# Output projection in 256-wide operands, partial sums added off TensorE, and one unit for the value products

## The chip, the cores and the metric

The kernel runs on one core of a Trainium2 chip. The metric is the device time of one execution in microseconds: the median of three runs, with the lowest and the highest beside it. TensorE (PE) does the matmuls, VectorE (DVE), ScalarE (ACT) and GpSimd (POOL) the elementwise work, and SyncE (SP) issues nearly all DMAs.

## The reference

Two attention layers over the same 2048 x 512 input `x` (bf16), mixed row by row by a gate. Layer A is a recurrence over 64 segments of 32 tokens; layer B is causal attention inside four blocks of 512 tokens, with a running memory.

```python
g = sigmoid((x * gate_w).sum(-1, keepdims=True))

# A: 32 heads of 128, M = 8 memory rows, seg_len = 32
mem = mem0
for s in range(64):
    h = concat([mem, x[:, 32*s : 32*s + 32]], axis=1)     # 40 rows of 512
    q, k, v = h @ Wq, h @ Wk, h @ Wv                      # 32 heads x 128
    p = softmax(where(mask, q @ k.T * 128**-0.5, -1e9))   # 40 x 40 a head
    o = einsum('bhte,hed->btd', p @ v, Wo)                # 40 rows of 512
    mem = o[:, :8]
    outs.append(o[:, 8:])
a = concat(outs)

# B: 32 heads of 16, blocks of 512 tokens, softmax attention plus a linear memory
b = (...) @ wo
out = g * a + (1 - g) * b
```

The 40 rows of a segment are the eight memory rows and its 32 tokens; the first eight rows of the segment's output are the memory of the next one. So the segments of A can only run one after the other.

## The kernel before

`build` (L258) records operations for each engine in the order in which Python emits them, and `Prog.emit` (L211) turns the recorded reads and writes into semaphore waits. Each engine runs its own list in order. For layer A the order is written out by hand: sixteen lists `A_LIST0` to `A_LIST15`, one for each group of four segments, in which a word such as `2.K0x` is one unit of work of segment 2 of the group. `plan_a` (L1275) makes the units and runs the lists.

A segment's TensorE work has 32 columns: its eight memory rows and its first 24 tokens, held in `hT` (two buffers, one a segment; GpSimd copies the tokens in, `x_copy`, L1554). The last eight tokens of four segments are 32 more columns, done once a group from `xL` (`left_units`, L1327; `ol_units`, L1422); no later segment needs them early. With 32 columns a matmul uses a quarter of the array's columns, so four matmuls run side by side, on row quarters `SEG * j` of one PSUM bank.

Units of one segment, in the order in which they depend on each other (`b` is 0 or 1, one half of the 32 heads):

- `K`, `Q`, `V` + `b` + `x` or `y` (`nat_pass`, L1566, matmuls at L1305): the projections, 512 columns a matmul, eight matmuls a unit; `x` needs the first half of the memory rows in `hT`, `y` the second. `k`, `q`, `v` copy them out of PSUM, `TK`, `TQ` transpose them on VectorE (L1317).
- `S` (L1592): the scores, `X` exp on ACT, `Y` the mask on VectorE, `M` the sums of each row by a matmul with ones (L1633), `L` logarithm and exp on ACT for the reciprocal (L1640, L1643), `N` and `n` the normalising on VectorE and GpSimd (L1647, L1653).
- `PV`, `PL` (L1656, L1669): the value products of one half, into two pairs of banks, for the segment's own tokens and for the left ones. `E` + `b` + `a` or `b` copies two banks at a time to `OT_sb` (L1681).
- `W` + `b` + `a` or `b` (`wo`, L1690): Wo, eight matmuls of 512 columns a unit (`out_part`, L1386, matmuls at L1392). Each of the four row quarters of the bank sums other heads, so four partial sums of 32 rows x 512 stand in one bank.
- `H0`, `H1` copy the halves of the bank to `WF` in float32; `F0`, `F1` (`fold`, L1403, matmuls at L1410) add the four partial sums and transpose them by a float32 matmul with a stacked identity; `hm0`, `hm1` (L1705) copy the memory columns to the other `hT`, `ax0`, `ax1` (L1711) the other columns to `aT_st`. At the end of a group VectorE transposes `aT_st` into rows, and four DMAs store them in DRAM (L1463).

Layer B (`BAttn`, L869) and the last quarter of its projections (`LateB`, L789) are cut into small units too (`bS` scores, `bE` exp and mask, `bP` values, `bT` the end of a job, `pj` and `pp` late projections), and these and the units of the left tokens stand between the units of A. The tail units `tb`, `tf` (L1482) load A's rows back, make B's rows (L1505) and store `g * a + (1 - g) * b`. SP issues the loads for B (`load`, L889), the stores and the tail's loads from one queue in order.

PSUM has eight banks. `Banks` (L43) hands them out while the list is run; `pair` gives two neighbours, and where no bank is free, `relief` runs a pending unit first.

Of the kernel before, what the change touches and what calls it, by code (L numbers as in the profile page):

```python
# [42 lines left out]
class Banks:  # L43
# [3 lines left out]
    def __init__(self, res):  # L47
        self.free = list(range(len(res)))
        self.res = res
        self.oldest = True  # L50
        self.relief = lambda: False

    def take(self, long=False):
        while not self.free and self.relief():
            pass
        assert self.free, "out of banks"
        f = self.free
        if long:
            c = [b for b in f if b < 2] or f
        elif self.oldest:  # L60
            c = [b for b in f if b > 1] or f
        else:
            whole = [b for b in f if b > 1 and b ^ 1 in f]
            c = [b for b in f if b not in whole and b > 1] if len(whole) <= 4 else [b for b in f if b > 1]
            c = c or [b for b in f if b > 1] or f
        b = c[0]
        f.remove(b)
        return b

    def pair(self):  # L70

        found = lambda: [(max(self.free.index(b), self.free.index(b + 1)), b) for b in self.free if b % 2 == 0 and b + 1 in self.free]
        while not found() and self.relief():
            pass
        c = found()
        c = [x for x in c if x[1] > 1] or c
        assert c, "no two neighbouring banks"
        b = min(c)[1]
        self.free = [k for k in self.free if k not in (b, b + 1)]
        return [b, b + 1]  # L80
# [177 lines left out]
def build(nc, es, A_x, A_mem0, A_Wq, A_Wk, A_Wv, A_Wo, B_wq, B_wk, B_wv, B_wo, B_beta, gate_w, out, dbg=None):  # L258
# [31 lines left out]
    def alloc(stack, *specs):  # L290
        at, spans = 0, {}
        for name, shape, dt, n in specs:
# [10 lines left out]
    alloc(es, ("ident", [128, 128], BF16, 0), ("xT", [128, C, S], BF16, 0), ("hT", [128, C, SEG], BF16, 2),  # L303
          ("Wk_sb", [128, C, HE], BF16, 0), ("Wq_sb", [128, C, HE], BF16, 0), ("Wv_sb", [128, C, HE], BF16, 0),
          ("Wo_sb", [128, H, DM], BF16, 0), ("woB_sb", [128, C, DM], BF16, 0),
          ("gw_sb", [128, C], BF16, 0), ("g_sb", [128, NTT], F32, 0), ("omg_sb", [128, NTT], F32, 0),
# [6 lines left out]
          ("aTg", [128, C, 128], BF16, 0), ("fold", [128, SEG], F32, 0), ("VNL", [128, 2, 512], BF16, 0),  # L313
          ("WF", [128, DM], F32, 0))
    esP = ExitStack()
    in_p = alloc(esP, ("wkB", [128, C, DM], BF16, 0), ("wqB", [128, C, DM], BF16, 0), ("phK", [128, 4, DM], BF16, 0), ("etmp", [128, 512], BF16, 5),
# [4 lines left out]
    v.x_sb = v.Wo_sb[:, 0:NTT, :]  # L321
    v.wvB = v.woB_sb
# [7 lines left out]
          ("oTt", [128, 16, 32], F32, 0), ("t1_sb", [128, DM], F32, 0), ("aT_st", [128, C, 128], BF16, 2))  # L330
# [11 lines left out]
    dram("aTd", [NG, 128, DM])  # L342
# [4 lines left out]
    def Rs(name):  # L347
        if name not in R:
            R[name] = Res(name)
            home = v.home(name)  # L350
            if home:
# [5 lines left out]
             ("QT", "QT_sb"), ("VN", "V_sb"), ("Pn", "P_sb"), ("P0", "P_sb"), ("P1", "P_sb"), ("R0", "R_sb"), ("R1", "R_sb"), ("OTL", "OTL"),  # L357
             ("OT", "OT_sb"), ("oTt", "oTt"), ("t1", "t1_sb"), ("aT", "aT_st"))

    def late_home(name):  # L360
        if name.startswith(("aTd", "aTg", "PT")):
# [4 lines left out]
        return h + name[3] if h == "aT_st" else h  # L366
# [27 lines left out]
    v.g_out = [P.group("out%d" % i, "out") for i in range(NG)]  # L394

# [32 lines left out]
    v.BK.oldest = False  # L428
    v.BK.free = sorted(v.BK.free)
    plan_a(v, NSEG_RUN)  # L430
    for go in v.g_out:
# [9 lines left out]
def plan_const(v):  # L441
# [29 lines left out]
    def late():  # L471
# [7 lines left out]
        rf = Rs("fold")  # L479
        gp(lambda g: g.memset(v.fold[:], 0.0), rf, "fold0", True)  # L480
        for j in range(4):
            sel(v.fold[:], [[-1, SEG]], ALU.not_equal, 1.0, -SEG * j, 1, rf, "fold1_%d" % j)
# [17 lines left out]
def plan_warm(v):  # L500
    P, Rs, BK = v.P, v.Rs, v.BK
    v.warm = v.WF[:, :].bitcast(BF16)[:, 0:512]
# [12 lines left out]
def plan_loads(v, A_x, A_mem0, A_Wq, A_Wk, A_Wv, B_wq, B_wk, B_wv, B_wo, B_beta, gate_w):  # L515
# [35 lines left out]
    def wo(q):  # L551
        P.dma(v.grp("Wo%d" % (q // 2)), lambda s: s.dma_start(v.Wo_sb[:, 4 * q:4 * q + 4, :], wosrc[:, 4 * q:4 * q + 4, :]),
              writes=[Rs("Wo%d" % (q // 2))] + ([Rs("x_sb%d%d" % (q, h)) for h in range(2)] if q < 4 else []), name="dma_Wo%d" % q)
# [70 lines left out]
def gate_parts(v):  # L624
# [4 lines left out]
    def dots(k):  # L629
# [4 lines left out]
        def f_gate(pe):  # L634
            ins = None
            for i in range(4 * k, 4 * k + 4):
                for c in range(C):
                    ins = pe.matmul(v.pb[bk][:, i:i + 1], v.xT[:, c, i * 128:(i + 1) * 128], v.gw_sb[:, c:c + 1],
                                    start=(c == 0), stop=(c == C - 1), skip_group_check=True)
            return ins  # L640
        P.op("pe", f_gate, reads=x_res(v, k) + [Rs("gw")], writes=[v.rbank[bk]], name="gate_mm%d" % k)
        if k == NTT // 4 - 1:
            sigmoid(v, v.pb[bk][:, 0:NTT], v.g_sb, v.omg_sb, "g", [v.rbank[bk]])
            BK.give(bk)

    def memory():
# [8 lines left out]
        v.evac("dve", v.hT[0][:, :, 0:v.M], v.pb16[bk][:, 0:C * v.M].rearrange("p (c t) -> p c t", t=v.M), [bk], [Rs("hTm0_0"), Rs("hTm0_1")], "memT0")  # L655
# [133 lines left out]
class LateB:  # L789
# [25 lines left out]
    def project(self):  # L815
# [23 lines left out]
        P.op("pe", f, reads=x_res(v, v.NB - 1) + [Rs("wvB" if m == "V" else "woc%d" % (k % 4))], writes=[v.rbank[bk]], name="lp%d_%d" % (k, half))  # L839
# [4 lines left out]
    def finish(self):  # L844
# [9 lines left out]
        if k == 0:  # L854
            P.op("gp", lambda g: g.memset(self.vst[:, :, 16:17], 1.0), writes=[Rs("t1")], name="v17l")
# [3 lines left out]
                  self.vst[:, :, 0:16].rearrange("p (e m) d -> p m e d", e=2), "t1", "vd%d_%d" % (sb, i)),  # L859
# [9 lines left out]
class BAttn:  # L869
# [45 lines left out]
    def scores(self):  # L915
# [8 lines left out]
        bks = v.BK.pair() + v.BK.pair()  # L924
# [134 lines left out]
A_LIST0 = """  # L1059
    ixl wl 0.Q0x iKL0x iQL1x iQL0x 0.K0x 0.Q0y iQL0 0.K1x 0.K1y 0.q0 0.TQ0 iKL0 0.xc iQL0e 0.K0y iKL0e~ iKL1x 0.k1 bS wl bE bE bE iQL1 wl bE 0.k0~ iKL1 pj  # L1060
# [823 lines left out]
```

## Time and profile before

| what | value |
|---|---|
| runs | 832.05 us median, 831.28 to 834.23 |
| profiled execution, span | 828.9 us, 3.15 below the median of the runs |
| TensorE clock granted | 1.000 |
| matmuls | 21,947 |
| DMA | 57.48 MB, mean 69 GB/s; 329 to 419 GB/s in the first three slices of 40 |

By stage the engines were busy so (us of each stretch):

| stretch | PE | DVE | ACT | POOL | GB/s |
|---|---|---|---|---|---|
| 0 to 50 | 46.29 | 23.96 | 27.78 | 22.72 | 378 |
| 50 to 100 | 46.12 | 29.25 | 33.98 | 14.50 | 206 |
| 400 to 500 | 98.04 | 74.32 | 75.61 | 36.00 | 39 |
| 760 to 829 | 64.05 | 42.73 | 39.03 | 12.78 | 40 |

The span is the time from the first to the last instruction on the core; the runs' times hold what lies around it as well. The weights come in during the first 50 us while the projections of B run; the recurrence of A starts at 50 us and ends 5 us before the end. A line of a group reads: line of code, engine, operation, output and inputs, shapes and count, then busy time and the mean of one in ns, then the idle time before it and what ended it. A row of the chain or of the timeline begins with its start and its length in us.

### The profile page before, as it was taken

To read this page: it belongs to the slowest core of one execution; us is meant where nothing else is said; L and a number is where in the kernel's file an instruction comes from. 1 tells how busy PE (TensorE), PEld (TensorE's weight loads), DVE (VectorE), ACT (ScalarE), POOL (GpSimd) and SP (SyncE) were. 2 spreads that over 40 slices of the span, in tenths; PEclk is the share of its full clock that TensorE was granted. 3 is DMA by queue.
4 is the path that set the end of the run, shared out by engine and by line. 5 is a ranking of instruction groups with operands and counts; after the bars stand their busy time and mean duration, and the time that the engine had idled before them with its cause. 6 is when DMAs were issued, how large, how long until landed. Compare 5 with 4: busy or idle time off the path is not lost.

```text
span 828.9 us, 49046 instructions
## 1 busy us (share of the span) xinstructions
PE 804.7 (97%) x21947; PEld 433.6 (52%) x21947; DVE 575.6 (69%) x1392; ACT 592.2 (71%) x1510; POOL 287.6 (35%) x780
## 2 busy tenths in 40 slices
PE   8998999999999999999999999999999999999998
PEld 4544555555445555555555555554555555555544
DVE  4555666577677777687777777877777777677656
ACT  5557777777776867777777777677777686777654
POOL 4613333433333333434342333433333333334111
PEclk9999999999999999999999999999999999999999
DMA  8997312212011121111102121211102111210111
GB/s 329 419 374 223 87 36 62 47 26 60 19 38 36 31 50 27 44 37 47 38 19 46 30 50 32 47 38 46 37 21 50 27 49 33 47 36 17 43 27 47
DMA packets 98257, 57.48 MB, mean 69 GB/s; under 512 B 71800, under 2 KB 92160, under 8 KB 96512
## 3 DMA queue, kind: packets, MB, share of 16 engines
q1 hardware_dynamic: 97488, 53.58, 22.3%
q8 instruction: 172, 2.82, 1.4%
q10 hardware_dynamic: 560, 0.79, 0.3%
q14 instruction: 37, 0.30, 0.1%
HBM read 37.14 MB, written 17.20 MB: 66 GB/s over the span
## 4 chain that ended last, share of the span: by engine, by line
PE 81%; ACT 7%; DMA 5%; DVE 3%; issue 1%; POOL 1%; SPq 0%; ACTq 0%; DVEq 0%; POOLq 0%
PE ps L1305 44%; PE ps L1392 17%; PE ps L1410 4%; PE ps L1663 3%; PE ps L933 2%; PE ps L986 2%; DMA scr_mzd<-MZ 2%; PE ps L1505 2%; DMA scr_kqd<-stgk 2%; PE ps L1598 2%; PE ps L1633 1%; ACT PT L954 1%; PE ps L699 1%; ACT R_sb L1643 1%; ACT WF L390 1%
## 5 line engine op out<-in xcount | busy, mean ns | idle before, releaser
L960 POOL TENSOR_SCALAR_AFFINE_SELECT PT<-PT 128x128 bf16<-128x128 bf16 (+2 forms) x320 | 117.3, 367 | 204.5 <-ACT PT L954 163.5
L954 ACT ACTIVATE PT<-ps 128x512 bf16<-128x512 f32 x320 | 176.1, 609 | 5.8 <-PE ps L933 3.9
L1305 PE MATMUL ps<-Wq_sb,hT 128*32 128x512 bf16 x2048 | 139.4, 379 | 0.5
L1305 PE MATMUL ps<-Wv_sb,hT 128*32 128x512 bf16 x2048 | 137.6, 379 | 0.1
L1305 PE MATMUL ps<-Wk_sb,hT 128*32 128x512 bf16 x2048 | 136.9, 379 | 0.2
L1392 PE MATMUL ps<-Wo_sb,OT_sb 128*32 128x512 bf16 x2048 | 127.4, 380 | 0.0
L1653 POOL TENSOR_TENSOR P_sb<-P_sb,R_sb 128x64 bf16<-128x64 bf16 x128 | 50.9, 398 | 144.8 <-ACT R_sb L1643 140.9
L390 ACT ACTIVATE OT_sb<-ps 128x320 bf16<-128x320 f32 x167 | 67.9, 434 | 22.8 <-PE ps L1675 21.7
L1305 PEld LDWEIGHTS ps<-Wk_sb,hT 128*32 128x32 bf16 x2048 | 59.7, 97 | 45.8 <-ACT hT L390 2.6
L1305 PEld LDWEIGHTS ps<-Wq_sb,hT 128*32 128x32 bf16 x2048 | 59.3, 97 | 45.8 <-ACT hT L390 2.3
L1317 DVE STREAM_TRANSPOSE QT_sb<-QN_sb 128x256 f32<-128x256 f32 x128 | 56.1, 440 | 24.2 <-ACT QN_sb L390 22.0
L1392 PEld LDWEIGHTS ps<-Wo_sb,OT_sb 128*32 128x32 bf16 x2048 | 48.1, 96 | 45.7 <-ACT OT_sb L390 6.4
L1317 DVE STREAM_TRANSPOSE KT_sb<-KN_sb 128x256 f32<-128x256 f32 x128 | 55.9, 439 | 21.6 <-ACT KN_sb L390 18.8
L390 ACT ACTIVATE QN_sb<-ps 128x512 bf16<-128x512 f32 x83 | 49.9, 602 | 28.4 <-PE ps L1305 27.5
L390 ACT ACTIVATE WF<-ps 128x256 f32<-128x256 f32 x97 | 32.8, 381 | 51.6 <-PE ps L1392 51.5
L1612 ACT ACTIVATE P_sb<-ps 128x224 bf16<-128x224 f32 x128 | 45.9, 360 | 27.8 <-PE ps L1603 17.2
L390 ACT ACTIVATE KN_sb<-ps 128x512 bf16<-128x512 f32 x79 | 47.0, 599 | 25.7 <-PE ps L1305 24.8
L1305 PEld LDWEIGHTS ps<-Wv_sb,hT 128*32 128x32 bf16 x2048 | 50.7, 95 | 27.6 <-issue 1.3
L392 DVE CAST OT_sb<-ps 128x320 bf16<-128x320 f32 x89 | 42.9, 488 | 26.0 <-PE ps L1675 25.5
L392 DVE CAST V_sb<-ps 128x512 bf16<-128x512 f32 x82 | 55.9, 683 | 4.0 <-PE ps L1305 3.1
L1647 DVE TENSOR_TENSOR P_sb<-P_sb,R_sb 128x160 bf16<-128x160 bf16 x128 | 42.2, 329 | 20.1 <-ACT R_sb L1643 18.4
L1663 PEld LDWEIGHTS ps<-P_sb,V_sb 32*128 32x128 bf16 x2048 | 23.0, 91 | 54.4 <-DVE P_sb L1647 27.9
(139 smaller groups left out, 1484.7 us busy)
## 6 DMA issues: line engine op xcount, KB each, us to landing
Wk_sb<-in_A_Wk_dram SPq DMA_DIRECT2D x4, 1024.0 KB, 9.8
Wq_sb<-in_A_Wq_dram SPq DMA_DIRECT2D x4, 1024.0 KB, 13.7
Wv_sb<-in_A_Wv_dram SPq DMA_DIRECT2D x4, 1024.0 KB, 16.6
Wo_sb<-in_A_Wo_dram SPq DMA_DIRECT2D x8, 512.0 KB, 6.1
scr_vld<-VNL SPq DMA_DIRECT2D x16, 256.0 KB, 2.3
VL<-scr_vld SPq DMA_DIRECT2D x64, 64.0 KB
scr_kqd<-stgk SPq DMA_DIRECT2D x12, 256.0 KB, 9.6
Vj<-scr_vd SPq DMA_DIRECT2D x32, 68.0 KB, 2.4
```

Source lines behind the costliest of these rows:

```text
L390: P.op("act", lambda a: a.activation(dst, src, ACT.Copy), reads=[v.rbank[k] for k in bks], writes=dres, name=name)
L392: P.op("dve", lambda d: d.tensor_copy(dst, src), reads=[v.rbank[k] for k in bks], writes=dres, name=name)
L954: P.op("act", lambda a: a.activation(pt, v.pb[bk], ACT.Exp, scale=v.SCALE_B), reads=[v.rbank[bk]], writes=[rp], name="be%d_%d" % (n, t))
L960: P.op("gp", lambda g: g.affine_select(mv, mv, [[0, len(cut)], [1, 128]], ALU.is_ge, 0.0, base=0, channel_multiplier=-1), reads=[rp], writ ...
L1305: ins = pe.matmul(pb[bk][SEG * j:SEG * (j + 1), :], lhs(c), cols(w, j) if split else w[:, 512 * j:512 * (j + 1)], start=(c == 0), stop=(c ...
L1317: P.op("dve", lambda d: d.transpose(to, src), reads=reads, writes=writes, name=name)
L1392: ins = pe.matmul(pb[bk][SEG * j:SEG * (j + 1), :], lhs(4 * k + j), Wo_sb[:, 4 * k + j, :], start=(first and k == ks[0]), stop=False, skip ...
L1410: ins = pe.matmul(pb[bk][SEG * j:SEG * (j + 1), SEG * n:SEG * (n + 1)], cols, v.fold[:, :], start=True, stop=True, skip_group_check=True)
L1612: P.op("act", lambda a: a.activation(P_sb[:, b, :], pb[bk][:, 0:224], ACT.Exp, scale=SCALE), reads=[rbank[bk]], writes=[Rs("P%d" % b), Rs( ...
L1647: P.op("dve", lambda d: d.tensor_tensor(wide(P_sb, b)[:, :, 0:L], wide(P_sb, b)[:, :, 0:L], R_sb[:, b, :].rearrange("p (i q) -> p i q", q= ...
L1653: P.op(ENG["n"], lambda d: d.tensor_tensor(left(P_sb), left(P_sb), grp04(R_sb[:, b, :]), ALU.mult), reads=[Rs("R%d" % b)], writes=[Rs("P%d ...
L1663: ins = pe.matmul(pb[bks[j]][:, L * i:L * (i + 1)], V_sb[SEG * j:SEG * (j + 1), b, i * E:(i + 1) * E], P_sb[SEG * j:SEG * (j + 1), b, LW * ...
```

## The change

Wo (`out_part`): a row quarter no longer takes all 512 columns of its own heads. Quarters 0 and 1 take the two column halves of heads 0 to 15, quarters 2 and 3 those of heads 16 to 31. So two partial sums of 32 rows x 512 stand in 64 + 64 partitions and 256 columns of a bank, made by 64 matmuls of 256 columns a segment where there were 32 of 512. `k` picks four heads of each half.

```diff
-                for j in range(4):
-                    ins = pe.matmul(pb[bk][SEG * j:SEG * (j + 1), :], lhs(4 * k + j), Wo_sb[:, 4 * k + j, :],
-                                    start=(first and k == ks[0]), stop=False, skip_group_check=True)
...
+            for n in range(4):
+                for j in range(4):
+                    h = 16 * (j // 2) + 4 * k + n
+                    ins = pe.matmul(pb[bk][SEG * j:SEG * (j + 1), 0:256], lhs(h), Wo_sb[:, h, :].rearrange("p (k q c) -> p q k c", q=2, c=64)[:, j % 2],
+                                    start=(first and not n), stop=False, skip_group_check=True)
```

The memory: `fold`, its constant and its matmuls are gone, and with them `H` in two halves before the fold, `hm`, `ax`, `aT_st` and the group's transpose. `hm` is now four VectorE instructions from the bank to the columns of `x` itself: `xTp` holds eight memory rows in front of the tokens, the memory of segment `s + 1` is written over the last eight tokens of segment `s`, and a segment's 32 columns lie in one piece. `hT` and GpSimd's `x_copy` are gone.

```diff
+        def w_mem():
+            src = pb[wb["bk"]][:, 0:256].rearrange("p (k q n) -> p k n q", k=4, n=2)
+            P.op("dve", lambda d: d.transpose(v.tt[:, :, :].rearrange("p (k n) t -> p k n t", n=2), src), ...)
+            P.op("dve", lambda d: d.tensor_copy(v.tu[0:64, :, :], v.tt[64:128, :, 0:M]), ...)
+            for b in range(2):
+                dst = xTp[64 * b:64 * b + 64, :, SEG * (s + 1):SEG * (s + 1) + M].rearrange("p (a n) t -> p a n t", n=2)
+                one, two = (t[0:64, :, 0:M].rearrange("p (a b n) t -> p b a n t", a=2, b=2)[:, b] for t in (v.tt, v.tu))
+                P.op("dve", lambda d, dst=dst, one=one, two=two: d.tensor_tensor(dst, one, two, ALU.add), ...)
```

The other rows: `G` and `H` copy the two partial sums to `WF0` and `WF1` (64 x 256, float32, ACT or VectorE), `ws` adds them on GpSimd into bf16 rows and stores these with one DMA a segment. The left tokens' Wo goes the same way (`O` units `0` to `3`, `e`, `f`, `s`).

```diff
+    def half_out(bk, i, eng, name):
+        evac(eng, v.WF[i][0:64, :], pb[bk][64 * i:64 * i + 64, 0:256], [bk], [Rs("WF%d" % i)], name)
+
+    def sum_rows(dst, res, name):
+        P.op("gp", lambda gq: gq.tensor_tensor(dst[0:64, :], v.WF[0][0:64, :], v.WF[1][0:64, :], ALU.add), reads=[Rs("WF0"), Rs("WF1")], writes=[res], name=name)
+
+    def rows_out(dst, src, reads, res, grp, name):
+        P.dma(grp, lambda sp: sp.dma_start(dst, src), reads=reads, writes=[res], name=name)
```

The tail loads A's rows with eight DMAs a group instead of one. The last segment's Wo (`out_whole`) lets each quarter take all heads and 128 columns, so that no sum is left; its rows are mixed with the gate straight from PSUM (`finz`) and stored by four DMAs, without the transposing matmuls of before (L1538).

The values: one unit `PV` does both halves, into four banks, each of which holds the heads of both halves for one quarter; `E0` to `E3` copy one bank each to `OT_sb`, and `W0` to `W3` take the heads of one bank each.

```diff
-        def pv_main(b):
-            bks = held[b] = B.pair() + B.pair()
...
+        def values():
+            bks = held[0] = B.four()
...
+            P.op("pe", f_main, reads=[Rs("VN0"), Rs("VN1"), Rs("Pm0"), Rs("Pm1")], writes=[rbank[k] for k in bks], name="pv%d" % s)
...
+            P.op("pe", f_left, reads=[Rs("VL%d_%d" % (par, b)) for b in range(2)] + [Rs("PL0"), Rs("PL1")], writes=[rbank[k] for k in bks], name="pvL%d" % s)
...
+        def ot_ev(j):
+            bk = held[0][j]
+            evac(ENG["E%d" % j], OT_sb[:, :, :].rearrange("p (b j i) q -> p j b (i q)", j=4, b=2)[:, j], pb[bk][:, 0:8 * L].rearrange("p (b w) -> p b w", b=2),
+                 [bk], [Rs("OT%d" % j)], "OTev%d_%d" % (s, j))
+            B.give(bk)
```

The lists: one list `A_ORDER` for all 64 segments takes the place of the sixteen. Every word of it runs exactly its unit; `relief`, `pair` and units that run only if they can are gone. The stretch around the values of segment 29, as an example:

```
29.M0 bP 29.L1 29.L0 29.n1 L8.QL0x 29.v0 O6.1 29.n0 29.N1 29.N0 29.PV 28.H L8.QL0y 29.E1 29.E0 29.E3 29.E2 29.W0 29.W1 29.W2 29.W3 L8.QL0e bS 29.hm
```

The built programs hold 21,947 recorded matmul passes before (each float32 matmul counts twice) and 22,011 matmuls after.

More of the change, by code (lines that the diff above doesn't have):

```diff
@@ L49, in __init__ @@
         self.res = res
-        self.oldest = True
-        self.relief = lambda: False
     def take(self, long=False):
-        while not self.free and self.relief():
-            pass
         assert self.free, "out of banks"
         f = self.free
[L58 to L65, printed above, removed]
+        c = [b for b in f if (b < 2) == long] or f
         b = c[0]
@@ L68, in take, with four @@
         return b
[L70 to L80, printed above, removed]
+    def four(self):
+        return [self.take() for _ in range(4)]
     def give(self, *bks):
@@ L1589, in segment @@
         head = lambda t, h: t[:, h // 2, :, h % 2]
+        wide = [heads4(P_sb[:, b, :]) for b in range(2)]
+        So = 4 * LW
         def scores(b):
@@ L1854 @@
+    for u in (DEV.get("order") or A_ORDER).split():
+        v.swap = u[-1] == "~"
+        units[u.rstrip("~")]()
+    assert bat.pv_n == bat.total and not bat.late and late.q == len(late.work) and not wo_left
 _INS = ['A_x', 'A_mem0', 'A_Wq', 'A_Wk', 'A_Wv', 'A_Wo', 'A_seg_len', 'B_x', 'B_wq', 'B_wk', 'B_wv', 'B_wo', 'B_beta', 'gate_w']
```

878 lines of the change are left out of this document (358 added, 520 removed).

## Prediction

> **What bounds the kernel now.** I read the page's busy line first, then the chain of waits, then the groups of instructions, and last the timeline of TensorE, segment by segment.
>
> ```profile
> PE 804.7 (97%) x21947; PEld 433.6 (52%) x21947; DVE 575.6 (69%) x1392; ACT 592.2 (71%) x1510; POOL 287.6 (35%) x780
> PE ps L1305 44%; PE ps L1392 17%; PE ps L1410 4%; PE ps L1663 3%; PE ps L933 2%; PE ps L986 2%; DMA scr_mzd<-MZ 2%; PE ps L1505 2%; DMA scr_kqd<-stgk 2%; PE ps L1598 2%; PE ps L1633 1%; ACT PT L954 1%; PE ps L699 1%; ACT R_sb L1643 1%; ACT WF L390 1%
> ```
>
> TensorE is busy 97% of the span, but a busy matmul is not a matmul at its pace: one 512-wide matmul is drawn 380 ns long while sixteen of them start within 0.86 us, 53.8 ns each. So I counted every matmul in the instruction order of the kernel and gave it the pace at which its kind follows itself in the timeline: 53.8 ns for 512 wide, 217 where all 128 columns of the array are used, 6.6 and 6.3 for the two kinds of scores, 12.5 for the sums, 6.9 for the values, 8.3 for a pass of the fold, 27 to 41 for attention B. That makes 755 us, against a span of 828.9: 74 us are waits hidden in the 97%. The first projection of segment 0 starts at 50.0 us, segment 4 starts at 112.3, the last Wo matmul ends at 824.06; from segment 4 on, a segment takes 11.86 us, of which 10.9 are matmuls.
>
> The second view is the serial path of one segment, in the chain of waits near the end:
>
> ```profile
> 799.64 1.87 PE ps L1392 x32
> 801.50 0.02 issue
> 801.53 0.39 ACT WF L390
> 801.92 0.04 issue
> 801.96 0.61 PE ps L1410 x32
> 802.57 0.03 issue
> 802.60 3.64 PE ps L1305 x64
> 806.24 0.10 PE ps L1598 x16
> ...
> 808.20 0.20 ACT R_sb L1640
> 808.41 0.02 issue
> 808.43 0.34 ACT R_sb L1643
> 808.77 0.02 issue
> 808.80 0.34 DVE P_sb L1647
> 809.13 0.05 issue
> 809.18 0.27 PE ps L1663 x16
> ```
>
> A segment cannot start its projections (L1305) before the memory of the one before has gone through Wo (L1392), the copy out (WF), the fold (L1410) and the copy into hT. What the timeline gives for the five places where this path leaves TensorE (segments 3 to 62; fastest / mean; in brackets the other matmuls that stand there in the order, at their pace): last K or Q projection to the second scores 1.34 / 1.64 (1.58); scores to second sums 1.03 / 1.31 (1.25); second sums to second values 1.31 / 1.76 (1.42); values to Wo 0.13, nothing needed, since Wo begins with the heads of the other half; last Wo to the next projection 1.28 / 1.50 (1.14). The brackets sum to 5.39 and the fastest waits to 4.96: there is just enough other work to cover the path. The kernel is bound by matmuls, and loses 0.95 us a segment where work and wait don't meet.
>
> **The change, part by part.**
>
> Folds gone. 64 segments and 16 groups, 2,560 passes:
>
> ```profile
> L1410 PE MATMUL ps<-fold,WF 128*32 128x32 f32 x2048 | 37.7, 199 | 6.0 <-ACT WF L390 2.2 <-ACT hT L390 1.1 <-issue 0.9
> L1410 PE MATMUL ps<-fold,LN_sb 128*32 128x32 f32 x512 | 7.3, 197 | 0.0
> ```
>
> At 8.3 ns a pass (a run of 31 takes 0.25 us to the next matmul) this is 21 us of pace, not the 45 of the busy column.
>
> Wo at 256. 64 matmuls of 256 columns take the place of 32 of 512, plus as many weight loads more. The 256-wide rows of the same 32-column form are those of L1505 at the end of the chain, sixteen of them beside eight 512-wide ones:
>
> ```profile
> 820.11 0.43 PE ps L1305 x8
> ...
> 825.17 0.44 PE ps L1505 x16
> ```
>
> So 1.72 us before and after: nothing. The bound above is L986, twelve in 0.41: 34 ns, 0.45 us a segment more; I take L1505, the same form.
>
> Values in one unit. The four L1675 matmuls are followed by the next matmul only after 0.13 us, where their own pace is 0.04: leaving the 32-row form costs some 0.1. One such change a segment instead of two saves 6 us. But TensorE now waits for the normalising of both halves, and then, before the first Wo, for the first copy of OT: end of matmul 0.19, copy 434 ns (ACT, OT_sb), 0.11 back, 0.74 in all. Before, this copy lay beside the other half's values.
>
> The memory. WF copy (381 ns), fold and hT copy (186) become four VectorE instructions in a row: a transpose out of PSUM (L1317, 128x256 f32: 440), a copy of 64x64 and two adds of 64x32. For the last three the rows are small VectorE instructions, 165 (hT copy) to 233 ns (128x64). With 0.19 in front, three gaps of 25 ns and 0.08 back to TensorE: 1.29 to 1.5; I take 1.30 (170 ns each, 64x32 being nearest the hT copies), and 0.03 for what follows: 1.33. The Q/K/V projections wait for it, and behind it on VectorE stand the copies of Q, K and V.
>
> The adds have two inputs in SBUF, and GpSimd gets 79 adds more. The timeline shows such a pair meeting:
>
> ```profile
> 408.48 0.41 POOL L1748 COPY QT_sb<-QTL 128x256 bf16<-128x256 bf16 x1
> 408.49 0.58 DVE L1647 TENSOR_TENSOR P_sb<-P_sb,R_sb 128x160 bf16<-128x160 bf16 x1 [0.24 <-ACT R_sb L1643]
> ```
>
> L1647 takes 325 ns otherwise. Over all, L1616 and L1647 started behind a running GpSimd instruction take 0.03 to 0.06 longer on the mean, 0.3 at worst. With GpSimd running 40% of the time (below) two adds pay 2 x 0.4 x 0.04 = 0.03. The Trainium skill, "SBUF — State Buffer", section "Who interferes with whom", has a stronger form: a VectorE instruction with two SBUF inputs is shut out for the whole GpSimd instruction. The mean of the rows bears out a small part of that; what it would make of the time is the third rival.
>
> Engines. VectorE: 63 x 0.44 + 189 x 0.17 + 64 x 0.42 for the new work, less aT_st, hT, WF, LN and aT transposes (47), V copies up 19, Q and K down 22: 576 to about 606 us, 74%. ACT drops to about 560. GpSimd loses the x copies (18 us) and gains 79 adds at 0.40 (128x64) to 0.75 us (128x256 f32): at 0.75 about 329, 40%. None becomes the bound. The copies to WF and GpSimd's adds feed only stores, and hide beside the next segment; WF has one buffer a half, so a late add holds the next copy and the Wo bank, but 0.38 + 0.75 us stand against a period of 11.7. GpSimd's masks for B queue behind an add: 0.75 us at most, with B's values behind them.
>
> DMAs: SP issues 626 instead of 495, at 0.33 to 0.63 us each, 66 us more on a queue that spends most of its time waiting. The row stores wait for GpSimd, and B's key loads (L901) queue behind them; a late load would starve the fill, by up to one 0.75 us add. I cost it at nothing: loads land in 1.9 us and are a segment ahead.
>
> The end: after the last Wo (824.06) come two folds, two brow units, L1538 and its copy, 2.1 us to 826.17; the new end is one VectorE instruction from PSUM, about 0.55 with its hand-over. 1.5 us saved. The start: the first eight segments hold 100.5 us of matmuls against 101.2: equal.
>
> **The sum.** The new order holds 734 us of matmuls, 10.5 a segment from segment 4 on with the values' saving. But the cover shrinks: the same five places now hold 1.26, 1.01, 1.04, 0.73 (with 0.26 of the left values' own time) and 1.01, less than any of the fastest waits. So a segment is no longer bound by matmuls but by its path. K and Q with the little that stands among them 3.55; 1.40 to scores 0.16; 1.06 to sums 0.10; 1.37 to values 0.24; 0.74 to Wo 1.78; 1.33 to the next: 11.73 us. The waits lie a little above the fastest of before. Against 11.86 this is 0.13 x 62 = 8 us less; with the end 1.5, the span is 819.3. The runs' median lies 3.15 above the span of before: **822 us**.
>
> **The rivals.**
>
> All cover holds: the loss a segment stays as it is, and 21 + 6 + 1.5 us come off 832.05: 804. For it: TensorE is 97% busy, and the loss of now came in spite of enough cover. Against: every gap of the new order is shorter than its wait.
>
> The longer path decides, slower: joining the values puts a full wait for both normalisings and one for the OT copy in a row, which other work covered before. If the first three waits lie where the fastest quarter of before ends (1.44, 1.12, 1.51), with 0.80 and 1.40 for the two new ones, the path is 12.10, 0.24 more than now: + 15 - 1.5, 846. It decides from 11.88 on, 0.15 above my path, so queueing of 0.03 at each place is enough. For it: the means of before lie 0.2 to 0.4 above the fastest, and ACT is still above 65% busy. Against: part of those means is the cover itself.
>
> The memory's adds shut out: each add starts while a GpSimd instruction runs 40% of the time and sits out half of one as long as 0.75 us, 0.15 an add, 0.30 a segment instead of 0.03. Path 12.00: + 9 - 1.5, 839. For it: the 0.58 us row. Against: most pairs in the timeline pay a tenth of that.
>
> No change: path and matmuls give and take 8 us, 828 to 836, as when the memory's chain takes 1.45.
>
> **Chances.** Forecast 40, all cover holds 13, slower path 26, adds shut out 9, no change 12 in 100. About 0.5% (4 us) is what a measurement can tell from none. The forecast's own range is 815 to 829, a sliver of it inside 0.5%: faster 0.50, same 0.15, slower 0.35. The range for 8 in 10 runs from just under the full saving, 803, to the slower path, 846.
>
> **What would show it.** Right: no L1410; Wo runs of 16 at 0.43 us; TensorE's idle above 24 us, put down to OT and to the memory adds; segments of 11.7. If the adds are near 0.3 us, or values wait for P_sb longer than 1.4 after the sums, the slower path holds. If the idle stays at 24 us, all cover holds. B's scores waiting for DMA would be wrong in a way not foreseen.

## The result and the profile after

The changed kernel takes 861.5 us (861.0 to 862.2) where the kernel before took 832.4 beside it: a ratio of 1.035 (95% interval 1.033 to 1.037), slower by 29 us where 822 was forecast. The profiled execution has a span of 859.5 us, 30.6 more than before. Its TensorE clock was 0.995 on the mean, against 1.000: in two stretches of some 3.4 us, one in segment 0 and one from 615.2 us on in the middle, it was at half, which can explain at most 1.7 us each.

The page after, busy time and then the chain that ended last, by engine and by line:

```profile
PE 794.1 (92%) x22005; PEld 445.9 (52%) x22011; DVE 615.5 (72%) x1525; ACT 572.8 (67%) x1326; POOL 322.8 (38%) x790
PE 58%; DVE 13%; ACT 11%; DMA 7%; POOL 4%; issue 4%; SPq 3%; ACTq 0%; POOLq 0%; DVEq 0%
PE ps L1255 32%; PE ps L1342 13%; POOL PT L945 2%; ACT PT L939 2%; PE ps L1569 2%; DVE tt L1606 2%; DVE xTp L1611 2%; DVE V_sb L376 2%; PE ps L918 2%; ACT R_sb L1548 2%; PE ps L971 2%; DMA Wv_sb<-in_A_Wv_dram 2%; DVE P_sb L1552 2%; DMA scr_kqd<-stgk 2%; PE ps L1505 1%
```

TensorE is idle 65 us, not 24, and its part of the chain fell from 81% to 58%. VectorE's rose from 3% to 13%. The groups that are new there, from the instructions of VectorE by shape (busy, mean ns of one | idle before):

```profile
L1606 DVE STREAM_TRANSPOSE tt<-ps 128x256 f32<-128x256 f32 x63 | 28.3, 449 | 50.8 <-PE ps L1342 50.0
L1611 DVE TENSOR_TENSOR xTp<-tt,tu 64x32 bf16<-64x32 f32 x126 | 24.7, 196 | 3.0
L1607 DVE COPY tu<-tt 64x64 f32<-64x64 f32 x63 | 12.6, 200 | 2.2
```

And one segment's boundary in the chain of waits (start us, us, what):

```profile
600.83 0.34 DVE P_sb L1552
601.17 0.04 issue
601.21 0.37 PE ps L1569 x32
601.59 0.10 PE ps L1580 x8
601.68 0.55 PE ps L1255 x8
602.23 0.02 issue
602.25 1.96 PE ps L1342 x64
604.21 0.03 issue
604.24 0.46 DVE tt L1606
604.70 0.02 issue
604.72 0.36 DVE tu L1607
605.08 0.02 issue
605.11 0.18 DVE xTp L1611
605.29 0.01 issue
605.30 0.20 DVE xTp L1611
605.50 0.04 issue
```

Between Wo (L1342) and the next projection nothing of TensorE lies on the chain any more: four VectorE instructions in a row. (The copy L1607 is longer here than its mean; the last section comes back to this case.)

Where the time came from. I cut the execution at the projections of segments 0, 8 and 56 and at the end of the last Wo, and set the matmuls of the order, at the paces of the prediction, against the time:

| stretch | before | after | difference | of it matmuls | of it waiting |
|---|---|---|---|---|---|
| segments 0 to 7 | 113.0 | 120.4 | +7.4 | -0.8 | +8.2 |
| 8 to 55 | 570.8 | 582.9 | +12.1 | -18.8 | +30.9 |
| 56 to the last Wo | 90.3 | 101.9 | +11.6 | -1.2 | +12.8 |
| after it | 4.8 | 3.9 | -0.9 | | |

The matmuls fell by 21 us as counted. The waiting rose by 52. Not all of the shift comes from the folds and the values: the new list also places part B elsewhere. Of its 320 exponentials 246 stood in segments 8 to 55 and now 226 do; the first eight segments hold 68 where they held 58, the last eight 26 where they held 16. So the middle has less of B's work to put into its waits, and both ends have more.

### The profile page after: what moved, and what is told of

It is laid out like the page before. It is cut to its first block, busy times and chain, and to the rows that moved or that the text cites. A ratio compares the mean times of both kernels' runs of the same rounds, so it can differ in the third digit from the quotient of the medians.

```text
span 859.5 us, 49189 instructions
## 1 busy us (share of the span) xinstructions
PE 794.1 (92%) x22005; PEld 445.9 (52%) x22011; DVE 615.5 (72%) x1525; ACT 572.8 (67%) x1326; POOL 322.8 (38%) x790
## 4 chain that ended last, share of the span: by engine, by line
PE 58%; DVE 13%; ACT 11%; DMA 7%; POOL 4%; issue 4%; SPq 3%; ACTq 0%; POOLq 0%; DVEq 0%
PE ps L1255 32%; PE ps L1342 13%; POOL PT L945 2%; ACT PT L939 2%; PE ps L1569 2%; DVE tt L1606 2%; DVE xTp L1611 2%; DVE V_sb L376 2%; PE ps L918 2%; ACT R_sb L1548 2%; PE ps L971 2%; DMA Wv_sb<-in_A_Wv_dram 2%; DVE P_sb L1552 2%; DMA scr_kqd<-stgk 2%; PE ps L1505 1%
## 5 line engine op out<-in xcount | busy, mean ns | idle before, releaser
L1255 PE MATMUL ps<-Wv_sb,xTp 128*32 128x512 bf16 x2048 | 145.3, 379 | 0.1
L1255 PE MATMUL ps<-Wq_sb,xTp 128*32 128x512 bf16 x2048 | 137.0, 380 | 5.4 <-DVE xTp L1611 3.8
L1255 PE MATMUL ps<-Wk_sb,xTp 128*32 128x512 bf16 x2048 | 137.1, 380 | 4.3 <-DVE xTp L1611 3.4
L1342 PE MATMUL ps<-Wo_sb,OT_sb 128*32 128x256 bf16 x4032 | 123.7, 275 | 3.7 <-ACT OT_sb L374 3.0
L1342 PEld LDWEIGHTS ps<-Wo_sb,OT_sb 128*32 128x32 bf16 x4032 | 102.9, 97 | 27.3 <-ACT OT_sb L374 23.7
L1255 PEld LDWEIGHTS ps<-Wq_sb,xTp 128*32 128x32 bf16 x2048 | 55.3, 97 | 63.1 <-DVE xTp L1611 13.0
L1255 PEld LDWEIGHTS ps<-Wk_sb,xTp 128*32 128x32 bf16 x2048 | 55.6, 97 | 61.2 <-DVE xTp L1611 8.9
L374 ACT ACTIVATE QN_sb<-ps 128x512 bf16<-128x512 f32 x91 | 54.2, 599 | 44.0 <-PE ps L1255 43.4
L376 DVE CAST V_sb<-ps 128x512 bf16<-128x512 f32 x101 | 69.3, 687 | 6.9 <-PE ps L1255 5.9
L1606 DVE STREAM_TRANSPOSE tt<-ps 128x256 f32<-128x256 f32 x63 | 28.3, 449 | 50.8 <-PE ps L1342 50.0
L1363 POOL TENSOR_TENSOR WN<-WF 64x256 bf16<-64x256 f32 x63 | 46.0, 730 | 26.7 <-ACT WF L374 14.4
L1523 DVE TENSOR_TENSOR P_sb<-P_sb,mkeep 128x224 bf16<-128x224 bf16 x128 | 37.3, 292 | 25.1 <-ACT P_sb L1519 23.2
L1255 PEld LDWEIGHTS ps<-Wv_sb,xTp 128*32 128x32 bf16 x2048 | 43.2, 95 | 18.1 <-issue 1.9
## 6 DMA issues: line engine op xcount, KB each, us to landing
Wv_sb<-in_A_Wv_dram SPq DMA_DIRECT2D x4, 1024.0 KB, 15.8
```

The lines of the kernel that those rows point to most:

```text
L374: P.op("act", lambda a: a.activation(dst, src, ACT.Copy), reads=[v.rbank[k] for k in bks], writes=dres, name=name)
L376: P.op("dve", lambda d: d.tensor_copy(dst, src), reads=[v.rbank[k] for k in bks], writes=dres, name=name)
L1255: ins = pe.matmul(pb[bk][SEG * j:SEG * (j + 1), :], lhs(c), cols(w, j) if split else w[:, 512 * j:512 * (j + 1)], start=(c == 0), stop=(c ...
L1342: ins = pe.matmul(pb[bk][SEG * j:SEG * (j + 1), 0:256], lhs(h), Wo_sb[:, h, :].rearrange("p (k q c) -> p q k c", q=2, c=64)[:, j % 2], sta ...
L1363: P.op("gp", lambda gq: gq.tensor_tensor(dst[0:64, :], v.WF[0][0:64, :], v.WF[1][0:64, :], ALU.add), reads=[Rs("WF0"), Rs("WF1")], writes= ...
L1523: P.op(ENG["y"], lambda d: d.tensor_tensor(P_sb[:, b, :], P_sb[:, b, :], mkeep[:, :], ALU.min), reads=[Rs("mkeep")], writes=[Rs("Pm%d" % b ...
```

## The experiments

The table gives each kernel's ratio to the kernel before with its 95% interval, and of its profiled execution the us from the first projection to the last Wo of segment 3, and then from Wo to Wo. Names with a_ are edits of the changed kernel, with b_ of the kernel before.

| kernel | ratio | 0-3 | 4-7 | 8-55 | 56-63 |
|---|---|---|---|---|---|
| before | 1 | 61.1 | 50.7 | 570.7 | 91.6 |
| after | 1.0348 [1.0327, 1.0369] | 69.3 | 49.9 | 582.9 | 103.2 |
| b_nofold | 0.9867 [0.9851, 0.9883] | 61.8 | 50.6 | 563.7 | 89.6 |
| b_bf16 | 0.9891 [0.9872, 0.9910] | 62.4 | 50.5 | 564.5 | 90.6 |
| b_pconst | 0.9990 [0.9969, 1.0011] | 62.0 | 50.6 | 571.2 | 91.9 |
| b_nofoldp | 0.9789 [0.9772, 0.9806] | 60.6 | 50.6 | 558.7 | 88.7 |
| a_pconst | 1.0222 [1.0201, 1.0244] | 68.6 | 50.0 | 573.7 | 100.6 |
| a_mem3 | 1.0256 [1.0224, 1.0287] | 68.1 | 49.3 | 575.6 | 106.9 |
| a_wconst | 1.0273 [1.0248, 1.0298] | 68.4 | 49.9 | 578.2 | 102.7 |
| a_wpconst | 1.0232 [1.0207, 1.0258] | 69.4 | 49.5 | 572.8 | 104.1 |
| a_halfpv | 1.0313 [1.0277, 1.0349] | 70.1 | 50.0 | 582.7 | 103.2 |
| a_noadd | 1.0304 [1.0276, 1.0331] | 69.1 | 49.8 | 576.8 | 105.0 |
| a_tail | 1.0350 [1.0321, 1.0378] | 67.7 | 50.0 | 580.8 | 105.7 |
| a_tail3 | 1.0325 [1.0307, 1.0343] | 68.7 | 50.0 | 582.8 | 101.9 |
| a_ends | 1.0486 [1.0439, 1.0533] | 77.8 | 53.1 | 581.5 | 102.6 |
| a_endspv | 1.0444 [1.0399, 1.0489] | 79.6 | 54.9 | 582.5 | 100.5 |
| a_start | 1.0407 [1.0367, 1.0446] | 71.9 | 50.8 | 582.8 | 107.2 |
| a_pjsmall | 1.0348 [1.0325, 1.0371] | 69.4 | 50.1 | 581.5 | 106.0 |
| a_bexp | 1.0394 [1.0355, 1.0433] | 70.1 | 50.0 | 582.8 | 106.8 |
| a_bstart | 1.0357 [1.0327, 1.0387] | 69.5 | 50.0 | 583.9 | 103.0 |

The last eight segments scatter by some 4 us among kernels that are alike there (103.0 to 107.2; segment 63 alone took 13.0 to 17.7), segments 8 to 55 by some 3 (580.8 to 583.9), so a stretch is read against that.

**What the folds were worth.**

```diff
-            fold(wb["f%d" % hf], hf, v.WF, "WF%d", "wf%d" % s)
+            pass    # b_nofold: hm and ax copy from WF
-("fold", [128, SEG], F32, 0) ... ("WF", [128, DM], F32, 0)
+("fold", [128, SEG], BF16, 0) ... ("WF", [128, DM], BF16, 0)    # b_bf16
-lhs = lambda c: hT[s % 2][:, c, 0:SEG]
+lhs = lambda c: Wk_sb[:, c, SEG * s:SEG * (s + 1)]    # b_pconst; b_nofoldp: this and b_nofold
-rx = lambda half: [Rs("hTx%d" % (s % 2)), Rs("hTm%d_%d" % (s % 2, half))]
+rx = lambda half: [Rs("Wk")]
```

> The kernel before, without the 126 folds of its segments (those of the groups' left rows stay): memory and rows are copied from the tile of partial sums, so they lack three of four partial sums. If the kernel before was bound by the number of its matmuls, the 17 to 21 us of the folds come off: 809 to 816 us. Rival (the folds lay in a wait that stays): 822 to 830 us.

> The kernel before with its folds in bf16 instead of f32 operands (the partial sums are rounded to bf16 before they are added). A fold matmul of 32 rows took 18 ns in f32; score matmuls of 40 columns in bf16 take 6.6 ns. Matmul-bound: 818 to 824 us, faster than both kernels. Rival (a fold's time is fixed cost or lies in the wait): 829 to 833 us.

> The kernel before, where the projections of the segments take their stationary operand from a slice of Wk instead of the tokens and the memory. In the changed kernel the same edit took 9 to 10 us. If the new addition of the memory made that wait dearer, the kernel before gains clearly less: 827 to 831 us. If the wait was as dear before: 821 to 825 us.

> The kernel before without the folds of its segments, and with the stationary operand of the segments' projections from a slice of Wk, so that no matmul waits for the memory at all. If the wait for the memory was covered in the kernel before and only shows once the folds no longer fill it: 810 to 816 us against the 823 us without folds alone. If the segment is held elsewhere: 819 to 824 us.

b_nofold falls to its rival: the 17 us of fold matmuls in the segments were worth 11. There the memory's wait lies bare in part, for taking it away as well gives 6.5 us more (0.9867 to 0.9789; its first forecast is missed by 0.8 us). Without the folds and without that wait 17.6 us come off, the folds' whole time: in part they stood in the wait for the memory and filled it. The same edit with the folds in place gives nothing at all (0.999), less than either theory said. That run does not take the whole wait away: its folds still wait for the copy WF and stand ahead of the next projections, and the first starts 0.97 us behind the last Wo matmul on the mean, as in the kernel before. b_bf16 keeps every step of the kernel before, lands 0.3 us above its forecast, and at 824.3 us is faster than both kernels.

**The wait for the memory behind Wo.**

```diff
-lhs = lambda c: xTp[:, c, SEG * s:SEG * (s + 1)]
+lhs = lambda c: Wk_sb[:, c, SEG * s:SEG * (s + 1)]    # a_pconst
-rx = x_res(v, s // 16) + [Rs("xt%d" % s), Rs("xu%d" % s)]
+rx = [Rs("Wk")]
-            P.op("dve", lambda d: d.tensor_copy(v.tu[0:64, :, :], v.tt[64:128, :, 0:M]), ...)
-for t in (v.tt, v.tu))
+for t in (v.tt, v.tt))    # a_mem3
```

> The changed kernel, where the projections of the segments take their stationary operand from a slice of Wk instead of the tokens and the memory: the wait between Wo and the next projection is gone, the output is other numbers, all other instructions are the same. TensorE lost 0.46 us a segment there. Path theory: 828 to 838 us. Rival (VectorE, in order, holds the next step just as long): 848 to 860 us.

> The changed kernel without the copy between the transpose and the two additions of the memory, whose second input is then the first once more, so that the memory lacks one of the two partial sums. The chain behind Wo is 0.2 us shorter in each segment. If its length sets the segment (order's cover 1.00 us, chain 1.36): segments 8 to 55 lose 6 to 9 us of 582.9, the time is 851 to 855 us. If the next wait takes it up: less than 3 us, 859 to 862 us.

By the whole time a_pconst falls to its rival, and a_mem3 misses the path theory by 0.8 us. In the middle a_mem3 takes off what the path theory asks to see, a_pconst about a third of it. Without the wait, segments 8 to 55 lose 9.2 of the 12.2 us by which they are longer than before; with one instruction less they lose 7.3. TensorE lost 0.46 us a segment behind Wo beyond what its order fills; a_pconst brings that to 0.16, but the loss ahead of the scores rises from 0.31 to 0.40. So a part of what is taken away is waited for again at the next place. In the kernel before the same edit was worth nothing with its folds and 6.5 us without them, so most of what this wait costs now comes with the folds gone. How much the new addition adds to that was not separated; that its length counts, a_mem3 shows.

**The wait for the values ahead of Wo.**

```diff
-lambda h: OT_sb[:, h, q], [Rs("OT%d" % k)]
+lambda h: Wk_sb[:, h % 4, q], []    # a_wconst; a_wpconst: this and a_pconst
```

> The changed kernel, where the Wo matmuls of the segments take their stationary operand from a slice of Wk instead of the values: the wait between values and Wo is gone, the output and the memory are other numbers. TensorE lost 0.26 us a segment there beyond what its order fills. Path theory: 843 to 850 us. Rival (the time goes to the next wait, behind Wo, where the memory is awaited): 856 to 862 us.

> The changed kernel with both edits at once: Wo's stationary operand and that of the segments' projections from a slice of Wk. One by one they took 5 and 9 us of segments 8 to 55 (582.9 to 578.2 and 573.7). If the two waits add: 567 to 570 us there, the time 844 to 848 us, still above the kernel before, since start and end stay. If one hides behind the other: 573 to 577 us, 850 to 853 us.

a_wconst misses the path theory by 6 us and lies at its rival's edge; a_wpconst adds nothing to a_pconst, as its second forecast had it. Even there the middle takes 572.8 us, 2 more than in the kernel before, with 19 us less of matmuls: some 21 of the 31 us of new waiting are still there, and no run says where. The trace shows why the first did not take the wait away (TensorE in order of time, with the idle time before an instruction and what ended it):

```profile
407.46 0.26 PE L1580 MATMUL ps<-P_sb,VL 32*128 32x64 bf16 x8
407.65 0.61 PE L1255 MATMUL ps<-Wq_sb,xL 128*32 128x512 bf16 x8
408.47 1.71 PE L1342 MATMUL ps<-Wo_sb,Wk_sb 128*32 128x256 bf16 x56 [0.21 <-ACT OT_sb L374]
```

Wo reads nothing of OT here and still waits for the copy of it: from the last value matmul of the segment's own tokens to the first of Wo it takes 0.84 us at the median, as in the changed kernel, and 0.92 on the mean, where that kernel has 0.98. Following `Banks` through the list, in 50 of 64 segments Wo's own PSUM bank is one of the four that the values filled and the copies empty; in 34 the values leave no bank free at all. So the copy stands ahead of Wo twice, by operand and by bank, and the experiment removed one.

```diff
-59.PV ... reads=[Rs("VN0"), Rs("VN1"), Rs("Pm0"), Rs("Pm1")]
+59.PV0 59.PV1 ... reads=[Rs("VN%d" % b), Rs("Pm%d" % b)]    # a_halfpv, every segment, same banks
```

> The changed kernel with the value products in two units again, one a half, in the same banks and at the same place: the first half's products stand in the gap in which TensorE waits for the second half's normalisation. If the joint unit lengthens the path (0.24 us of cover a segment missing between sums and values, where TensorE lost 0.45 us a segment): 848 to 855 us. If the gap is set by something else or is covered anyway: 859 to 863 us.

The second theory holds: by the ratios 3 us, within the intervals, and 0.2 us in segments 8 to 55. The joint unit as such is not the loss.

**GpSimd's additions.**

```diff
-half_out(wb["bk"], i, ENG["H%d" % i], "wev%d_%d" % (s, i)) ... sum_rows(WN, rw, "wsm%d" % s)
+evac(eng, WN[0:64, :], pb[bk][64:128, 0:256], [bk], [rw], name)    # a_noadd, for i = 1
```

> The changed kernel without GpSimd's 63 additions of the two row sums: the second half is copied straight to the output tile, so that the rows stored lack the first half. Adds theory (GpSimd's work is in the way of VectorE and of the stores): 850 to 856 us. Path theory (nothing on the path waits for them): 858 to 863 us.

The path theory's range holds it. The ratio is 0.4% lower, 4 us, and the intervals touch. But in the profiled execution, which was the fastest of the four by 2.5 us, segments 8 to 55 are 6.1 us shorter, more than the scatter there: GpSimd's additions do cost the middle something, and where was not followed up.

**The end of the list.**

```diff
-59.X1 T12.l 57.H ... 60.Q0x T12.f ... L15.VLt T13.l ... 61.X0 T13.f ... 62.ws T14.f
+59.X1 57.H ... L15.VLt T12.l ... 60.hm T12.f ... T13.l ... 61.hm T13.f ... 63.E1 T14.f    # a_tail3
+rows of groups 13 and 15 in oTs instead of aTg; a_tail: this and the final multiply-adds (f), the loads (l) of group 12 where they were
```

> The changed kernel; groups 13 and 15 finish in a second tile, and the final multiply-add of groups 12 to 14 stands up to a segment later in the list, so that VectorE no longer waits there for the eight row loads of a group. Tail theory (groups 14 and 15 lose 4 and 8 us because that wait holds the Q and K copies): 850 to 854 us. Path theory: 858 to 862 us.

> The changed kernel; only the end of its list is edited: the row loads of group 12 stand behind the reload of the left values, groups 13 and 15 finish in a second tile, and the final multiply-adds stand up to a segment later. Queue theory: segment 60 takes 11.5 to 12 us instead of 15.1, segments 56 to 63 99 to 101 us instead of 103.2, the time 857 to 860 us. If the loads are hidden anyway: segment 60 stays near 15, 861 to 863 us.

Segment 60 takes 15.1 us in the changed kernel, and 13.0 to 16.3 in the eleven variants that keep T12's loads where they are, a_tail among them. SP's queue there, after:

```profile
800.01 0.83 SPq L1415 DMA_DIRECT2D aTg<-scr_aTd  x1
800.89 0.70 SPq L1417 DMA_DIRECT2D aTg<-scr_aTl  x1
...
806.13 0.66 SPq L1417 DMA_DIRECT2D aTg<-scr_aTl  x1
806.84 0.50 SPq L1366 DMA_DIRECT2D scr_aTd<-WN  x1
807.38 0.58 SPq L1288 DMA_DIRECT2D scr_vld<-VNL  x1
...
809.70 2.51 SPq L1296 DMA_DIRECT2D VL<-scr_vld  x4
```

Eight row loads take 6.8 us to issue. Behind them stand the store of the left values (L1288) and their reload (L1296), for which this segment's value products wait; and on VectorE the final multiply-add waits for the loads with the Q and K copies behind it:

```profile
808.24 0.75 DVE L1458 SCALAR_TENSOR_TENSOR aTg<-aTg,g_sb,t_sb 128x512 bf16<-128x512 bf16 x1 [4.17 <-DMA aTg<-scr_aTl]
808.91 0.69 DVE L376 CAST QN_sb<-ps 128x512 bf16<-128x512 f32 x1
```

a_tail left these loads where they were and moved the multiply-add, and the segment stayed at 15.8. In a_tail3 the store and the reload go first (its list is printed on one line, so that line numbers are lower):

```profile
803.68 0.33 SPq L1112 DMA_DIRECT2D scr_vld<-VNL  x1
...
805.70 3.08 SPq L1120 DMA_DIRECT2D VL<-scr_vld  x4
808.83 0.83 SPq L1240 DMA_DIRECT2D aTg<-scr_aTd  x1
```

Segment 60 takes 11.6 us there, and 11.6 and 11.4 in the two kernels below that have the same edit: the queue theory holds for the segment. Segments 56 to 63 take 101.9 us, less saved than forecast, since segment 56, ahead of the edit, took 14.8 us for 13.2. Of the whole time 2 us of these 3.5 are left (1.0348 to 1.0325), and the intervals overlap.

**The start of the list.**

```diff
-0.K0x L0.QL1x L0.QL0x wl L0.VL0x L0.VL1x wl
+0.K0x L0.QL1x L0.QL0x wl pj pj pp~ pj pj pp~ L0.VL0x L0.VL1x wl    # a_ends, with a tail edit like a_tail3
+L0.VL*, 0.V0x behind the K and Q units; 3.qt bE 2.hm pp~    # a_start
+v.pb[bk][q, 0:64], v.xT[:, c, t0:t0 + 64] for late K, Q    # a_pjsmall
+activation(pt[:, 0:64], v.pb[bk][:, 0:64]) for n >= 146    # a_bexp; a_bstart: 4 <= n < 20, no mask
```

> The changed kernel, with two edits of its unit list ahead of segment 4: the value projections of segment 0 and group 0 stand behind those of K and Q, and a late-projection copy that waited for a store on VectorE stands behind the memory addition instead of ahead of it. Start theory (8 us of the 31 us were lost before segment 4, 4.7 of them as TensorE idle in segment 0): 853 to 857 us. Path theory (the loss is spread over all segments): 859 to 862 us.

> The changed kernel with edits of its list at both ends: four late value projections stand in segment 0 where TensorE waits 3.1 us for Wv; groups 13 and 15 finish in a second tile, the loads of group 12 stand behind the reload of the left values instead of ahead of it, the final multiply-adds up to a segment later. Start theory (segments 1 to 3 took 9 us more because work that segment 0 could hide in its waits stands there): segments 0 to 3 lose 2 to 4 us (69.3 to 65 to 67). Queue theory (segment 60 takes 15.1 us because VectorE and the left values wait behind eight row loads on SP's queue): segments 56 to 63 lose 3 to 5 us (103.2 to 98 to 100). Both: 853 to 857 us. Neither: 859 to 863 us.

> The kernel of the run before this with the value products in one unit a half, as the best version of the changed kernel. If both gains add: 850 to 855 us, and still slower than the kernel before, because the wait for the memory behind Wo (9 us) and that for the values ahead of it (5 us) stay. If the half units bring nothing: the same as the run before this.

In these two kernels the last groups also take rows of B that belong to a neighbouring group: the load of group 12's rows moved along.

> The changed kernel, where the late K and Q projections of part B (16 runs of 8 matmuls, nearly all in segments 1 to 3) are made over 64 of their 512 columns, so that the rest of their results is old data. That takes 6 us of matmuls out of these segments. If segments 1 to 3 are bound by matmuls: 43.4 us there fall to 37 to 39.5. If by waits: 42 to 44.

> The changed kernel, where 32 exponentials of part B in segments 1 to 4 are made over 64 of their 512 columns and their masks on GpSimd are left out, so that these products are partly old data and not masked. That takes some 12 us off ScalarE and as much off GpSimd there. If these two engines hold segments 1 to 3: 43.4 us fall to 38 to 41, the time to 857 to 860 us. If not: above 42.5 us, 861 to 864 us.

> The changed kernel, where the last 28 of part B's 320 exponentials are made over 64 of their 512 columns, so that the rest of those products is old data. Segments 56 and 57 hold 23 of them (the kernel before had 7 there). If ScalarE's share of part B stretches these two segments (13.2 and 13.6 us): they fall to 11.7 to 12.2 us, the time to 856 to 859 us. If not: they stay above 13 us and the time at 860 to 863 us.

None of the start's edits helped: a_start and a_ends came out slower than either of their theories, and a_endspv is the same as a_ends within the intervals. Busy time of the engines in segments 0 to 3, after and then before (stretch, length, then busy us of PE, PEld, DVE, ACT, POOL, the clock, the DMA share, GB/s):

```profile
50.40:76.30 25.90, 20.58 (x457) 10.37 (x459) 11.13 (x26) 10.24 (x24) 3.87 (x12) 0.93 0.95 304
76.30:88.90 12.60, 12.12 (x348) 6.65 (x344) 9.16 (x23) 8.79 (x21) 4.56 (x10) 1.00 0.17 47
88.90:103.40 14.50, 14.09 (x392) 7.72 (x384) 9.60 (x24) 10.53 (x23) 5.80 (x14) 1.00 0.40 101
103.40:119.70 16.30, 14.08 (x392) 7.27 (x388) 11.55 (x27) 11.33 (x25) 6.64 (x17) 1.00 0.24 64
```

```profile
50.00:77.00 27.00, 24.01 (x538) 11.57 (x537) 15.19 (x34) 15.89 (x33) 7.31 (x20) 1.00 0.98 316
77.00:88.30 11.30, 10.87 (x320) 5.37 (x320) 5.98 (x17) 8.19 (x20) 3.45 (x9) 1.00 0.36 90
88.30:100.30 12.00, 11.54 (x324) 6.36 (x321) 8.08 (x19) 9.91 (x25) 3.93 (x12) 1.00 0.28 67
100.30:111.10 10.80, 10.54 (x304) 4.95 (x306) 6.72 (x17) 6.76 (x17) 2.82 (x9) 1.00 0.18 52
```

Segment 0 lasts about as long in both kernels while the DMA engines are 95% busy with weights. The kernel before fills it with 24 us of TensorE work, 15 of VectorE and 16 of ScalarE; the changed one with less of each, and does the rest in segments 1 to 3, which take 9 us more. That is what the two tables show; what exactly holds segments 1 to 3 was not separated. Without 5 us of matmuls (a_pjsmall) or 12 us of ScalarE's and GpSimd's work (a_bstart) they stay at 42.7 and 42.4 us against 43.4; both together were not tried. Putting work back into segment 0 failed on SP's queue: in a_ends two stores of the late values waited there for VectorE,

```profile
61.47 4.95 SPq L849 DMA_DIRECT2D scr_vd<-t_sb  x2
66.47 0.44 SPq L532 DMA_DIRECT2D Wo_sb<-in_A_Wo_dram  x1
67.45 0.32 SPq L1112 DMA_DIRECT2D scr_vld<-VNL  x1
```

with the left values' store and loads of Wo behind them, and segment 0 took 36.7 us; segments 1 to 3 fell to 41.1. In a_start the left values came later, and their way through DRAM made TensorE wait 6.9 us. a_bexp: segments 56 and 57 took 14.3 and 13.8 us (13.2 and 13.6 in the changed kernel), so ScalarE's share of B is not what stretches them; this stays open.

## Why the prediction was wrong

The sum held the right parts and missed in three places. Against the profiled execution it was 18 us too low in segments 8 to 55 (6 less forecast, 12 more measured), 8 in the first eight segments, 13 in the last eight.

**The path of a segment: 11.73 forecast, 12.25 measured (segments 5 to 61).** That a segment is bound by its path and no longer by matmuls fits what was measured: in segments 8 to 55 the matmuls fell by 18.8 us, the time grew by 12.1, and a shorter path (a_mem3, a_pconst) took 7.3 and 9.2 of it off. The failed step is "the waits lie a little above the fastest of before". The five waits, in us:

| place | forecast | after, fastest | median | mean |
|---|---|---|---|---|
| K/Q to second scores | 1.40 | 1.34 | 1.44 | 1.51 |
| scores to second sums | 1.06 | 1.03 | 1.05 | 1.13 |
| sums to values | 1.37 | 1.31 | 1.36 | 1.47 |
| values to Wo | 0.74 | 0.78 | 0.84 | 0.98 |
| Wo to projection | 1.33 | 1.36 | 1.37 | 1.46 |

In the first three places the forecast lies near the median, in the two new ones below the fastest. "Values to Wo" runs from the last value matmul of the segment's own tokens; the prediction counted the left values' matmuls as work beside the copy, but they write the same four banks ahead of it, 0.08 us. A segment's length goes by the five means. They are 0.65 above the forecast in all, the medians 0.16, while the rest of the segment came out 0.1 shorter. With less cover than the fastest wait in every place, a late copy lengthens the segment. The rival "the longer path decides" is what happened in the middle, at 12.25 instead of its 12.10. (The 74 us that the prediction calls hidden in TensorE's 97% hold the 24 us that the page shows as idle; 50 are hidden.)

**The folds.** 21 us of pace are gone from the order, as counted; the sum by the path does not use them, the rival "all cover holds" does. In b_nofold 17 of them were worth 11: the count took no account of the wait that they filled, and a_pconst and b_nofoldp show that without the folds this wait lies bare.

**The start.** "Equal" was argued from the matmuls (100.5 against 101.2), and these were right. But segment 0 lasts 26 to 27 us in both kernels, with the DMA engines busy nearly all the time, so the work that the new list took out of it saved 1 us there, and segments 1 to 3, which hold it now, take 9 us more. Which part of that work costs them this stays open.

**The DMAs, "costed at nothing".** Wrong in the last groups: not B's loads, which were named, but the left values stand behind the row loads; 3.5 us in segment 60. The rest of the end's 11.6 us is not settled.

**What held.** Wo at 256: a segment's Wo matmuls start within 1.70 us on the mean, within 1.71 before. The memory's instructions: 449, 200 and twice 196 ns for 440 and three times 170, and 1.37 us at the median for 1.33. Engines: VectorE 615.5 for 606 (the terms as listed add up to 612), ScalarE 572.8 for 560, GpSimd 322.8 for 329. The end: 0.9 us saved for 1.5. The additions shut out by GpSimd cost as little as forecast, for another reason. The pair of L1611 takes 0.38 us in the 37 segments where GpSimd is idle and 0.44 on the mean, 0.90 at most, in the 26 where it runs: 0.02 a segment. But a mean hides what happens. In 20 of these GpSimd's instruction starts only when an addition is under way, and costs it nothing. In the six cases where an addition starts behind a running GpSimd instruction, it ends 0.04 to 0.05 us after that one, however long that takes:

```profile
144.53 0.72 POOL L1363 TENSOR_TENSOR OLN<-WF 64x256 bf16<-64x256 f32 x1
144.60 0.70 DVE L1611 TENSOR_TENSOR xTp<-tt,tu 64x32 bf16<-64x32 f32 x1
```

The stronger form in the Trainium skill's "SBUF — State Buffer", section "Who interferes with whom", says just this. The trace agrees in all six. So the third rival had the mechanism right and its frequency wrong: 6 of 126 additions start so, not 40 in 100, and the small mean that the prediction held against it is no evidence against the lock.

## What to carry to other kernels

Work that stands in a wait is worth less than its time, and what replaces it must be shorter than that wait or be covered by other work. When a change moves a loop from bound by one engine to bound by its path, price each wait by its mean under load, not by its fastest, and look for a second reason to wait, a bank, an in-order queue, behind the one that is removed. Where two engines may shut each other out, look at which starts first and when the other ends, case by case: the mean hides it. Count the start and the end of the list by what they wait for, not by their matmuls.

## What the runs showed of the hardware

The copy in the memory's chain, with a single input, is held up by GpSimd too. L1607 takes 190 ns in all 54 segments where GpSimd is idle at its start, and 258 on the mean, 460 at most, in the nine others. In the four of these nine where GpSimd's instruction had more than 0.14 us to go, the copy ends 0.04 to 0.05 us after it; in the other five it keeps its 190 ns. The transpose L1606, which reads PSUM, takes 450 ns with GpSimd running (14 cases) as with GpSimd idle. The Trainium skill, in the same section of "SBUF — State Buffer", counts copies among the operations that can take the ports shared with GpSimd; the trace agrees, at 0.07 us on the mean. One such case, three of its lines in order of time:

```profile
604.29 0.73 POOL L1363 TENSOR_TENSOR OLN<-WF 64x256 bf16<-64x256 f32 x1 [2.50 <-DVE WF L376]
604.44 0.11 PEld L1428 LDWEIGHTS ps<-woB_sb,oTg 128*32 128x32 bf16 x4
604.72 0.35 DVE L1607 COPY tu<-tt 64x64 f32<-64x64 f32 x1
```

Folds in bf16 instead of float32 have half as many matmuls in the record, 1,280 for 2,560, and took 9 us off the kernel before, nearly as much as leaving the segments' folds out (11; the intervals overlap).
